# The start of a fused attention and MLP kernel in another order: one tile alone, its q ahead of v's last part, and other slots for the work behind it

## The chip, the core and the metric

The kernel runs on one core of a Trainium2 chip. The time is the device's own, in microseconds (us), one launch, lower is better; runs of one kernel mostly agree within 0.3%. The profile's span runs from the first to the last instruction of the core and is about 2 us shorter than the time.

Engines: PE is TensorE (matmul), PEld its weight loads, DVE is VectorE, ACT is ScalarE, POOL is GpSimd, which also issues the loads that cast float32 to bfloat16. Each engine works through its own list in program order.

## The reference

```python
kv  = einsum('bhsd,bhse->bhde', k, v)             # B=8, H=8, S=576, D=64, float32
o   = einsum('bhsd,bhde->bhse', q, kv)
x   = o / sqrt(mean(o*o, -1) + 1e-6) * g_norm     # then heads side by side: [8, 576, 512]
xn  = (x - mean(x)) / sqrt(var(x) + 1e-6) * g_ln
out = x + relu(xn @ w_ch1) @ w_ch2                # w_ch1 [512, 2048], w_ch2 [2048, 512]
```

## The kernel before

Per batch there are four tiles of 128 rows (0 to 3), and the remaining 64 rows of two batches make one tile more. A tile goes through: o (PE), square (ACT), sum `ss` (DVE), root `rms` (ACT), x and the scaled, centred `xc` (DVE), a transpose of `xc` (PE, "turn") and its copy to `xT_blk` (ACT). Then come the two layers. The division by the standard deviation is put off to the output addition `finish`.

The first layer of a batch is 16 groups of 16 matmuls, the second 64 long matmuls. Each group, and each four long matmuls, opens a *slot*; an agenda says what else is issued just before a slot (the comments in the code cuts are put in here; `...` marks what is left out):

```python
    def tick():                                   # called at the head of each slot
        for _, fn in sorted(agenda.pop(clock[0], []), key=lambda e: e[0]):
            fn()
        clock[0] += 1
    ...
    at(4, lambda: turn_first(3, ps_m, "misc"))
    at(5, lambda: t[3].o())
    at(5.1, x3)                                   # tile 3: square, ss, root, y, x, xc
    at(6, lambda: t[2].turn(True))                # tile 2's transpose and its copy by ACT
    ...
    at(21, lambda: kv_of(1))
    q_turns(23, 1)                                # batch 1: DVE copies q, then PE turns it
    for j, s, tn in ((0, 24, 30), (1, 27, 34), (2, 31, 38), (3, 35, 42)):
        plan_tile(s, lambda j=j: main_tile(1, j), tn, True)
```

`plan_tile(s, ..., tn)` issues o, square and ss at slot s, root, y, x and xc at slot s + 2, and the turn at slot tn. Batch 0's first layer has slots 0 to 15, its second layer 16 to 31, batch 1's first layer begins at slot 32, and the groups of batch 1's tile 1 begin at slot 36.

```python
    for ts, c0, c1 in ((0, 0, 8), (1, 0, 8), (0, 8, 12), (1, 8, 12), (0, 12, 16), (1, 12, 16),
                       (2, 0, 16), (3, 0, 16)):
        mm1(0, ts, 1, c0, c1)                     # tile ts; four chunks of w1 to a slot
    ...
    for ts in range(4):
        mm2_part(0, ts, p2s[ts], 0, nDe // 2)
    for ts in range(4):
        ...
        mm2_part(0, ts, p2, nDe // 2, nDe)
        finish(0, ts, p2)                         # DVE: the output addition
```

The start loads k (float32, on two other queues), then on POOL's queue v in two halves, q of the lower rows in two halves of heads, w1's first chunk, and the rest. Tiles 0 and 1 go through the start together, in two halves of heads.

## Time and profile before

| | before |
|---|---|
| time, median of 4 | 291.75 us (291.61 to 292.32) |
| span | 289.6 us |
| TensorE busy | 281.9 us, 97% |
| first first-layer matmul of batch 0 | 15.78 us |
| second group of the first layer | 18.25 us in the timeline; 18.42 in the view of the chain (`--critical`), which counts it from the end of what went before |
| second layer of batch 0 begins | 33.37 us |
| first layer of batch 1 begins | 50.39 us |

The page of the kernel before, part 1: busy us, share, instructions.

```profile
span 289.6 us, 5791 instructions
PE 281.9 (97%) x2312; PEld 158.6 (55%) x2312; DVE 151.0 (52%) x335; ACT 155.0 (54%) x339; POOL 41.0 (14%) x68
```

The waits of PE in the kernel before: who waited for whom, in all, how often, the longest.

```profile
engine line waited for: us in total, times, longest us
PE even L219 <- DMA v_in<-in_v_dram: 1.4, 2, 0.7
PE p L196 <- DVE eps_sb L137: 1.2, 1, 1.2
PE tp L541 <- DVE xc L532: 0.8, 1, 0.8
PE o_ps L260 <- DVE qt L191: 0.2, 1, 0.2
```

Every wait in this view ends before 18.1 us, and PE is busy for 97% of the span. From there on the matrix unit sets the time of the whole kernel: what delays it once is not won back, and there is little to shorten but the start. The view leaves out waits under 0.15 us by its count.

The timeline of PE before (start us, busy us, what, count; in brackets the wait just ahead). L402 is the first layer, L418 the second, L337 a tile's turn:

```profile
15.78 1.34 PE L402 MATMUL p<-xT_blk,w_sb 128*128 128x128 bf16 x16
17.05 0.44 PE L183 MATMUL tp<-identity,q_in 64*64 64x64 bf16 x16
...
18.25 2.84 PE L402 MATMUL p<-xT_blk,w_sb 128*128 128x128 bf16 x48
21.03 0.44 PE L183 MATMUL tp<-identity,q_in 64*64 64x64 bf16 x16
...
23.42 0.39 PE L337 MATMUL tp<-identity,xc 128*128 128x128 bf16 x4
23.65 3.06 PE L402 MATMUL p<-xT_blk,w_sb 128*128 128x128 bf16 x48
26.64 0.31 PE L183 MATMUL tp<-identity,q_in 64*64 64x64 bf16 x8
...
33.37 4.48 PE L418 MATMUL p<-w_sb,m 128*128 128x512 bf16 x20
...
52.18 0.39 PE L337 MATMUL tp<-identity,xc 128*128 128x128 bf16 x4
```

The lines of L183 are turns of batch 0's q. The line at 23.42 is tile 2's turn at slot 6. Slots 6 and 7 are other tiles' groups, and tile 2's own start only at slot 8, so ACT has two slots (1.8 us) to copy the turned tile. The timeline of ACT before:

```profile
22.51 0.60 ACT L405 ACTIVATE m<-p 128x512 bf16<-128x512 f32 x1 [0.30 <-PE p L402]
23.00 0.59 ACT L266 ACTIVATE sq<-o_ps 128x512 f32<-128x512 f32 x1
24.34 0.30 ACT L297 ACTIVATE rms<-ss,eps_sb 128x8 f32<-128x8 f32 x1 [0.75 <-DVE ss L287]
24.55 0.58 ACT L405 ACTIVATE m<-p 128x512 bf16<-128x512 f32 x1
25.03 0.58 ACT L339 COPY xT_blk<-tp 128x512 bf16<-128x512 bf16 x1
```

Tile 3's square and root stand in ACT's list ahead of the copy, and ACT stands still for 0.75 us until DVE has the sum. The copy ends at 25.61, 2.2 us after the turn was issued. Two slots do not quite hide it: the 48 matmuls at 23.65 took 3.06 us, where the 48 at 18.25 took 2.84, so PE already loses about 0.2 us at tile 2's first group.

The timeline of DVE before, around batch 1's tiles (L423 is the output addition, L287 a sum, L292 begins a tile's y, L321 is its xc):

```profile
44.41 0.75 DVE L423 SCALAR_TENSOR_TENSOR o_sb<-p,rstd,x_blk 128x512 f32<-128x512 f32 x1 [1.09 <-PE p L418]
...
47.63 0.68 DVE L287 TENSOR_REDUCE ss<-sq 128x8 f32<-128x512 f32 x1
48.23 0.74 DVE L423 SCALAR_TENSOR_TENSOR o_sb<-p,rstd,x_blk 128x512 f32<-128x512 f32 x1
...
50.76 0.75 DVE L321 SCALAR_TENSOR_TENSOR xc<-x_blk,st_blk,g_ln_sb 128x512 bf16<-128x512 f32 x1
```

DVE has no gap there, but tile 1's xc ends at 51.51, still before its turn at 52.18.

### The profile page before, as it was taken

Reading aid. Unit: us, or ns where it says so; the run is one execution under the profiler, and the core shown is the slowest. Engines: PE = TensorE matmul, PEld = TensorE weight load, DVE = VectorE, ACT = ScalarE, POOL = GpSimd, SP = SyncE. Lnnn points to the kernel's source line nnn. Section 1 sums busy time; section 2 is a strip of 40 time slices with the busy share of each in tenths; the row PEclk is TensorE's granted clock in tenths of the full one; section 3 lists DMA queues with packets and bytes.
Section 4 is the critical chain, followed back from the end, with each engine's and each line's share of the span. In section 5 each row is a group of like instructions: output and inputs, shape, how many; then the busy total and the mean of one; then the engine's idle time right before and its main releaser. Section 6 shows DMA issues by size and latency. Waiting matters only on the chain.

```text
span 289.6 us, 5791 instructions
## 1 busy us (share of the span) xinstructions
PE 281.9 (97%) x2312; PEld 158.6 (55%) x2312; DVE 151.0 (52%) x335; ACT 155.0 (54%) x339; POOL 41.0 (14%) x68
## 2 busy tenths in 40 slices
PE   7889999999999999999999999999999999999995
PEld 2579755996569644444444444444444444444444
DVE  5775028847997793765366925762578300220022
ACT  3467755885469832882189418920894076016500
POOL 8522520032032003200410023000000000000000
PEclk9999999999999999999999999999999999999999
DMA  7999999469999918995997179938202510131033
GB/s 215 203 206 203 201 202 218 109 99 188 155 177 160 151 40 158 205 167 102 148 208 103 42 146 194 178 75 164 54 18 53 112 36 0 38 81 28 0 74 73
DMA packets 64378, 36.10 MB, mean 125 GB/s; under 512 B 31836, under 2 KB 59356, under 8 KB 64352
## 3 DMA queue, kind: packets, MB, share of 16 engines
q0 software_dynamic: 28016, 17.76, 44.2%
q1 hardware_dynamic: 35824, 17.25, 30.5%
q10 hardware_dynamic: 512, 0.72, 0.7%
q8 instruction: 18, 0.29, 0.4%
q14 instruction: 8, 0.07, 0.1%
HBM read 36.71 MB, written 9.44 MB: 159 GB/s over the span
## 4 chain that ended last, share of the span: by engine, by line
PE 93%; DMA 2%; ACT 1%; DVE 1%; POOL 1%; issue 1%; POOLq 0%
PE p L418 43%; PE p L402 43%; PE o_ps L260 3%; DMA q_in<-in_q_dram 2%; PE kv_ps L235 2%; PE tp L183 1%; PE p L196 1%; PE tp L337 1%; ACT sq L266 0%; PE tp L170 0%; PE o_half L500 0%; POOL v_in L126 0%; ACT xT_blk L542 0%; ACT m L405 0%; DVE x_blk L278 0%
## 5 line engine op out<-in xcount | busy, mean ns | idle before, releaser
L402 PE MATMUL p<-xT_blk,w_sb 128*128 128x128 bf16 (+2 forms) x1024 | 131.8, 286 | 0.2
L418 PE MATMUL p<-w_sb,m 128*128 128x512 bf16 (+2 forms) x608 | 129.2, 368 | 0.0
L405 ACT ACTIVATE m<-p 128x512 bf16<-128x512 f32 x144 | 85.5, 596 | 43.3 <-PE p L402 41.1
L402 PEld LDWEIGHTS <-w_sb 128*128 128x128 bf16 x1024 | 78.5, 98 | 44.1 <-issue 0.6
L418 PEld LDWEIGHTS <-m 128*128 128x128 bf16 x608 | 56.8, 98 | 61.8
L423 DVE SCALAR_TENSOR_TENSOR o_sb<-p,rstd,x_blk 128x512 f32<-128x512 f32 (+2 forms) x38 | 27.4, 721 | 54.3 <-PE p L418 48.7
L266 ACT ACTIVATE sq<-o_ps 128x512 f32<-128x512 f32 x34 | 20.2, 595 | 41.5 <-PE o_ps L260 41.4
L287 DVE TENSOR_REDUCE ss<-sq 128x8 f32<-128x512 f32 x34 | 23.0, 678 | 11.2 <-ACT sq L266 11.2
L329 ACT ACTIVATE dev<-x_blk,st_blk 128x512 f32<-128x512 f32 x36 | 25.7, 714 | 4.6 <-DVE st_blk L315 4.4
L321 DVE SCALAR_TENSOR_TENSOR xc<-x_blk,st_blk,g_ln_sb 128x512 bf16<-128x512 f32 x34 | 25.6, 752 | 1.2
L292 DVE TENSOR_TENSOR y<-o_ps,inv 128x512 f32<-128x512 f32 x34 | 23.5, 692 | 3.0
L311 DVE SCALAR_TENSOR_TENSOR x_blk<-y,g_norm_sb 128x512 f32<-128x512 f32 x34 | 23.5, 692 | 1.2
L411 DVE RECIPROCAL rstd<-rstd 128x4 f32<-128x4 f32 x9 | 1.6, 174 | 35.3 <-ACT rstd L410 35.3
L304 DVE RECIPROCAL inv<-rms 128x8 f32<-128x8 f32 x36 | 7.2, 201 | 23.0 <-ACT rms L297 23.0
L98 POOL COPY gate<-qt 1x1 bf16<-1x1 bf16 x5 | 0.9, 178 | 114.1 <-DMA qt<-q_p 114.1
L297 ACT ACTIVATE rms<-ss,eps_sb 128x8 f32<-128x8 f32 x36 | 10.7, 297 | 9.5 <-DVE ss L287 8.8
L260 PEld LDWEIGHTS <-qt 128*128 128x128 bf16 (+1 forms) x152 | 9.9, 100 | 7.4 <-issue 1.7
L260 PE MATMUL o_ps<-kv_pack,qt 128*128 128x128 bf16 (+1 forms) x152 | 13.3, 220 | 0.2 <-DVE qt L191 0.2
L196 PE MATMUL p<-fill_sb 128*128 128x512 bf16 x28 | 8.1, 445 | 1.2 <-DVE eps_sb L137 1.2
L329 ACT ACTIVATION_READ_ACCUMULATOR dev<-x_blk,st_blk 128x1 f32 x36 | 6.9, 190 | 0.0
L235 PEld LDWEIGHTS <-k_in 128*64 128x64 bf16 x280 | 5.0, 112 | 2.6 <-issue 2.5
L238 ACT CAST kv_pack<-kv_ps 64x256 bf16<-64x256 f32 x7 | 2.6, 366 | 7.2 <-PE kv_ps L235 7.2
(79 smaller groups left out, 116.8 us busy)
## 6 DMA issues: line engine op xcount, KB each, us to landing
out_dram<-o_sb SPq DMA_DIRECT2D x70, 128.0 KB, 2.4
w_sb<-in_moe_w_ch_dram POOLq DMA_DIRECT2D x8, 512.0 KB, 13.8
k_in<-in_k_dram POOLq DMA_DIRECT2D x7, 320.0 KB, 5.8
v_in<-in_v_dram POOLq DMA_DIRECT2D x7, 320.0 KB, 9.4
q_in<-in_q_dram POOLq DMA_DIRECT2D x7, 320.0 KB, 12.7
q_in<-in_q_dram POOLq DMA_DIRECT2D x8, 256.0 KB, 12.7
k_in<-in_k_dram POOLq DMA_DIRECT2D x7, 256.0 KB, 7.3
v_in<-in_v_dram POOLq DMA_DIRECT2D x7, 256.0 KB, 11.3
```

The costliest lines, as they stand in the source:

```text
L196: nc.tensor.matmul(p1, lhsT=fill_sb[:, :128], rhs=fill_sb, start=True, stop=True)
L260: nc.tensor.matmul(flat[rows, hp * 128:(hp + 1) * 128], lhsT=lhsT_of(hp), rhs=kvp[:, hp, :], start=True, stop=True)
L266: nc.scalar.activation(self.sq_t, self.o_ps, func=AF.Square)
L287: nc.vector.tensor_reduce(self.ss, self.sq_t, axis=AX.X, op=ALU.add)
L292: nc.vector.tensor_mul(self.y_t, self.o_ps, self.inv().to_broadcast([128, H, D]))
L311: nc.vector.scalar_tensor_tensor(x_blk[:, ts].rearrange("p (h d) -> p h d", h=H), in0=self.y_t, scalar=1.0, in1=g_norm_sb.to_broadcast([12 ...
L321: nc.vector.scalar_tensor_tensor(self.xc_t, in0=x_blk[:, self.ts], scalar=st[:, 1, self.ts:self.ts + 1], in1=g_ln_sb, op0=ALU.add, op1=ALU ...
L329: nc.scalar.activation(dev, x_blk[:, ts], func=AF.Square, bias=st[:, 1, ts:ts + 1], accum_out=st[:, 2, ts:ts + 1])
L402: nc.tensor.matmul(p1[:, i, :], lhsT=w1_sb[:, kk, de * 128:(de + 1) * 128], rhs=blk[2][:, kk, sl], start=(kk == 0), stop=(kk == nK - 1))
L405: nc.scalar.activation(m1[:, de0:de0 + per, sl], p1, func=AF.Relu)
L418: nc.tensor.matmul(p2[:, c0:c1], lhsT=m1s[b][:, de, ts * 128:(ts + 1) * 128], rhs=w2_sb[:, de, c0:c1], start=(de == 0), stop=(de == nDe - 1))
L423: nc.vector.scalar_tensor_tensor(o_sb[:, c0:c1], in0=p2[:, c0:c1], scalar=rstds[b][:, ts:ts + 1], in1=blks[b][0][:, ts, c0:c1], op0=ALU.mu ...
```

## The change

Intent: get tile 0 alone to the first layer early, by loading its part of q before v's last head pair; lay the other q turns into its waits; order the first layer by w1's chunks as they land; and load w2's third chunk ahead of batch 1's q, so that the second layer, now in three parts, does not wait for w2. Because q of batch 1 then lands later, its turns and the tiles behind move to later slots.

```diff
-    nc.gpsimd.dma_start(v_p[:, :HP // 2], pairs(v, 0, HP // 2))
-    nc.gpsimd.dma_start(v_p[:, HP // 2:], pairs(v, HP // 2, HP))
-    for h0 in (0, H // 2):
-        nc.gpsimd.dma_start(q_in[0][:64, h0:h0 + H // 2], lo(q, 0, h0, h0 + H // 2))
+    nc.gpsimd.dma_start(v_p[:, :HP - 1], pairs(v, 0, HP - 1))
+    nc.gpsimd.dma_start(q_in[0][:64, :, :2], lo(q, 0)[:, :, :2])
+    nc.gpsimd.dma_start(v_p[:, HP - 1:], pairs(v, HP - 1, HP))
+    nc.gpsimd.dma_start(q_in[0][:64, :, 2:], lo(q, 0)[:, :, 2:])
 ...
-    load_batch(1)
+    load(k_in[1], k, 1)
+    load(v_in[1], v, 1)
     load_w2(2)
+    load(q_in[1], q, 1)
     load_w2(3)
 ...   (kv of batch 0 in three pairs and one instead of two halves; tile 0 alone through the
 ...    start; tile 1's turn, o and square behind it, its sum behind tile 0's xc; turns of q for
 ...    tiles 2 and 3 ahead of slot 1; tile 2 takes the o_g path, in which
 ...    PE makes a second product with kv already times g_norm, and DVE needs one step less for x)
+    at(1, before_1)
+    at(2, before_2)                 # tile 2: o_g, root, x, xc
+    at(4, before_4)                 # tile 3: o, square, ss, root, y, x, xc
     at(6, lambda: t[2].turn(True))
 ...
-    q_turns(23, 1)
-    for j, s, tn in ((0, 24, 30), (1, 27, 34), (2, 31, 38), (3, 35, 42)):
+    q_turns(25, 1)
+    for j, s, tn in ((0, 26, 31), (1, 29, 34), (2, 32, 38), (3, 35, 42)):
 ...
-    for ts, c0, c1 in ((0, 0, 8), (1, 0, 8), (0, 8, 12), (1, 8, 12), (0, 12, 16), (1, 12, 16),
-                       (2, 0, 16), (3, 0, 16)):
+    for ts, c0, c1 in ((0, 0, 4), (1, 0, 4), (0, 4, 8), (1, 4, 8), (0, 8, 12), (1, 8, 12),
+                       (2, 0, 12), (0, 12, 16), (1, 12, 16), (2, 12, 16), (3, 0, 16)):
 ...
-    for ts in range(4):
-        mm2_part(0, ts, p2s[ts], 0, nDe // 2)
+    for de0, de1 in ((0, nDe // 2), (nDe // 2, nDe * 3 // 4)):
+        for ts in range(4):
+            mm2_part(0, ts, p2s[ts], de0, de1)
 ...
-        mm2_part(0, ts, p2, nDe // 2, nDe)
+        mm2_part(0, ts, p2, nDe * 3 // 4, nDe)
         finish(0, ts, p2)
```

More of the change, by code (lines that the diff above doesn't have):

```diff
@@ L191, in turn_first, with fill @@
         copy(qts[0][:, i, :, :n], tp[:, :, :n])
-    def fill(n, pool=ps2, tag="p2"):
+    def fill(n, p1=None):
+        if p1 is None:
+            p1 = ps2.tile([128, 512], f32, tag="p2", name="p1")
         for _ in range(n):
-            p1 = pool.tile([128, 512], f32, tag=tag, name="p1")
             nc.tensor.matmul(p1, lhsT=fill_sb[:, :128], rhs=fill_sb, start=True, stop=True)
-            del p1
+        return p1
     def turn_q_dma(b):
@@ L205, in turn_q_dma, with __init__, mms, copies @@
         qts[b] = q_t
-    def kv_first():
-        kvp = held[0] = kv_pack[0]
-        g = g_norm_sb.to_broadcast([128, HP // 2, D])
-        for i, (pe, te, po, to) in enumerate(((ps_m, "misc", ps1, "p1"), (ps1, "p1", ps1, "p1"))):
-            even = pe.tile([128, HP // 2, D], f32, tag=te, name="even")
-            odd = po.tile([128, HP // 2, D], f32, tag=to, name="odd")
-            hps = slice(i * HP // 2, (i + 1) * HP // 2)
-            for hp in range(hps.start, hps.stop):
+    class KvFirst:
+        def __init__(self, hp0, hp1, pools):
+            self.hps, self.pools = slice(hp0, hp1), pools
+        def mms(self):
+            n = self.hps.stop - self.hps.start
+            (pe, te), (po, to) = self.pools
+            self.even = pe.tile([128, n, D], f32, tag=te, name="even")
+            self.odd = po.tile([128, n, D], f32, tag=to, name="odd")
+            for hp in range(self.hps.start, self.hps.stop):
                 for j in range(JP):
                     js = slice(j * D, (j + 1) * D)
-                    for hh, dst in ((0, even), (1, odd)):
+                    for hh, dst in ((0, self.even), (1, self.odd)):
                         rows = slice(hh * D, hh * D + D)
-                        nc.tensor.matmul(dst[rows, hp - hps.start, :], lhsT=k_p[rows, hp, js],
-                                         rhs=v_p[rows, hp, js],
+                        nc.tensor.matmul(dst[rows, hp - self.hps.start, :],
+                                         lhsT=k_p[rows, hp, js], rhs=v_p[rows, hp, js],
                                          start=(j == 0), stop=(j == JP - 1))
-            nc.vector.tensor_copy(kvp[:D, hps, :D], even[:D])
-            nc.scalar.copy(kvp[D:, hps, D:], odd[D:])
-            nc.vector.tensor_mul(kv_g[:D, hps, :D], even[:D], g[:D])
-            nc.vector.tensor_mul(kv_g[D:, hps, D:], odd[D:], g[D:])
-            del even, odd
+        def copies(self):
+            nc.vector.tensor_copy(kv_pack[0][:D, self.hps, :D], self.even[:D])
+            nc.scalar.copy(kv_pack[0][D:, self.hps, D:], self.odd[D:])
+        def times_g(self):
+            g = g_norm_sb.to_broadcast([128, self.hps.stop - self.hps.start, D])
+            nc.vector.tensor_mul(kv_g[:D, self.hps, :D], self.even[:D], g[:D])
+            nc.vector.tensor_mul(kv_g[D:, self.hps, D:], self.odd[D:], g[D:])
+            del self.even, self.odd
     def kv_of(b):
@@ L474 @@
     qts[0] = qt_pool.tile([128, JJ, HP, 128], bf16, tag="qt", name="qt")
+    held[0] = kv_pack[0]
     fill(18)
-    kv_first()
-    t = [main_tile(0, i, ps2, "p2") for i in range(4)]
-    for i in range(2):
-        t[i].ss = work.tile([128, H, 1], f32, tag="ss", bufs=4, name="ss")
-    sqs = [work.tile([128, H, D], f32, tag="sq", name="sq") for _ in range(2)]
-    banks = (((ps_out, "ops"), (ps_m, "misc")), ((ps_out, "ops"), (ps1, "p1")))
-    copies = ((nc.scalar.copy, nc.scalar.copy), (nc.vector.tensor_copy, nc.vector.tensor_copy))
@@ L486, in half_turn @@
-    def half_turn(half):
-        hp0 = half * HP // 2
-        tps = [ps2.tile([128, HP // 2, 128], bf16, tag="p2", name="tp") for _ in range(2)]
-        for i in range(2):
-            turn_groups(tps[i], i, 2 * hp0, 2 * hp0 + H // 2)
-        for i in range(2):
-            copies[half][i](qts[0][:, i, hp0:hp0 + HP // 2], tps[i])
-    def half_o(i, half):
-        hp0 = half * HP // 2
-        pool, tag = banks[half][i]
-        o = pool.tile([128, H // 2, D], f32, tag=tag, name="o_half")
-        flat = o.rearrange("p h e -> p (h e)")
-        for k2 in range(HP // 2):
-            nc.tensor.matmul(flat[:, k2 * 128:(k2 + 1) * 128], lhsT=qts[0][:, i, hp0 + k2, :],
-                             rhs=kv_pack[0][:, hp0 + k2, :], start=True, stop=True)
-        nc.scalar.activation(sqs[i][:, half * H // 2:(half + 1) * H // 2], o, func=AF.Square)
@@ L504, in half_red @@
-    def half_red(i, half):
-        hs = slice(half * H // 2, (half + 1) * H // 2)
-        nc.vector.tensor_reduce(t[i].ss[:, hs], sqs[i][:, hs], axis=AX.X, op=ALU.add)
-    half_turn(0)
-    fill(2, ps_out, "ops")
-    half_o(0, 0)
-    half_turn(1)
-    half_o(1, 0)
-    half_o(0, 1)
-    half_red(0, 0)
-    half_red(0, 1)
-    half_o(1, 1)
-    t[0].root()
-    half_red(1, 0)
-    half_red(1, 1)
-    t[0].o_g(ps1, "p1")
+    kv_a = KvFirst(0, HP - 1, ((ps_m, "misc"), (ps1, "p1")))
+    kv_b = KvFirst(HP - 1, HP, ((ps1, "p1"), (ps1, "p1")))
@@ new lines, with part_o @@
+    t = [main_tile(0, 0)] + [main_tile(0, i, *((ps1, "p1") if i == 1 else (ps2, "p2")))
+                             for i in range(1, 4)]
+    t[0].ss = work.tile([128, H, 1], f32, tag="ss", bufs=4, name="ss")
+    sq_0 = work.tile([128, H, D], f32, tag="sq", name="sq")
+    o_0 = {}
+    def part_o(kv_x):
+        hp0, hp1 = kv_x.hps.start, kv_x.hps.stop
+        o_0[hp0] = ps_out.tile([128, 2 * (hp1 - hp0), D], f32, tag="ops", name="o_part")
+        flat = o_0[hp0].rearrange("p h e -> p (h e)")
+        for hp in range(hp0, hp1):
+            nc.tensor.matmul(flat[:, (hp - hp0) * 128:(hp - hp0 + 1) * 128],
+                             lhsT=qts[0][:, 0, hp, :], rhs=kv_pack[0][:, hp, :],
+                             start=True, stop=True)
@@ new lines, in part_sq, with part_red @@
+    def part_sq(kv_x):
+        hp0, hp1 = kv_x.hps.start, kv_x.hps.stop
+        nc.scalar.activation(sq_0[:, 2 * hp0:2 * hp1], o_0.pop(hp0), func=AF.Square)
+    def part_red(kv_x):
+        hs = slice(2 * kv_x.hps.start, 2 * kv_x.hps.stop)
+        nc.vector.tensor_reduce(t[0].ss[:, hs], sq_0[:, hs], axis=AX.X, op=ALU.add)
+    kv_a.mms()
+    kv_a.copies()
+    turn_first(0, ps2, "p2")
+    kv_a.times_g()
+    fill(2)
+    kv_b.mms()
+    kv_b.copies()
+    part_o(kv_a)
+    part_o(kv_b)
+    part_sq(kv_a)
@@ L521 @@
+    part_sq(kv_b)
+    kv_b.times_g()
+    part_red(kv_a)
+    part_red(kv_b)
+    turn_first(1, ps_m, "misc")
+    t[0].root()
+    t[0].o_g(ps2, "p2")
+    dead = fill(2)
+    t[1].o()
+    t[1].sq()
+    turn_first(J, ps_m, "misc")
     t[1].o_g(ps1, "p1")
-    fill(8)
+    fill(3, dead)
+    del dead
     t[0].x_g()
-    t[1].root()
     def halves_xc(i):
@@ L534, in halves_xc, with half_turn, before_1, before_2 @@
             yield xc
-    def halves_turn(i, xcs, pool, tag):
-        xT = t[i].blk[2]
-        for c, xc in enumerate(xcs):
-            tp = pool.tile([128, 2, 128], bf16, tag=tag, name="tp")
-            for kk in range(2):
-                nc.tensor.transpose(tp[:, kk, :], xc[:, kk * 128:(kk + 1) * 128], identity)
-            nc.scalar.copy(xT[:, 2 * c:2 * c + 2, i * 128:(i + 1) * 128], tp)
-    halves_turn(0, halves_xc(0), ps_out, "ops")
+    def half_turn(i, c, xc, copy):
+        tp = ps_out.tile([128, 2, 128], bf16, tag="ops", name="tp")
+        for kk in range(2):
+            nc.tensor.transpose(tp[:, kk, :], xc[:, kk * 128:(kk + 1) * 128], identity)
+        copy(t[i].blk[2][:, 2 * c:2 * c + 2, i * 128:(i + 1) * 128], tp)
+    for c, xc in enumerate(halves_xc(0)):
+        half_turn(0, c, xc, nc.scalar.copy)
+    t[1].red()
     t[1].x_g()
     xc1 = list(halves_xc(1))
-    def x2():
+    def before_1():
+        turn_first(2, ps_m, "misc")
+        tp = ps2.tile([128, HP, 128], bf16, tag="p2", name="tp")
+        turn_groups(tp, 3, 0, H)
+        half_turn(1, 0, xc1[0], nc.scalar.copy)
+        t[2].o()
+        half_turn(1, 1, xc1[1], nc.vector.tensor_copy)
+        t[2].sq()
+        nc.scalar.copy(qts[0][:, 3], tp)
         t[2].red()
-        t[2].y()
-        t[2].x()
+        del tp, xc1[:]
+    def before_2():
+        t[2].o_g(ps2, "p2")
+        t[2].x_g()
         t[2].xc()
-    def x3():
+    def before_4():
+        t[3].o()
         t[3].sq()
@@ L560, in x3 @@
         t[3].xc()
-    def o2():
-        t[2].o()
-        t[2].sq()
     def next_loads():
@@ L569, in next_loads @@
         load_batch(2)
-    at(1, lambda: turn_first(2, ps_m, "misc", nc.vector.tensor_copy))
-    at(1.1, lambda: halves_turn(1, xc1, ps_out, "ops"))
-    at(1.2, o2)
-    at(1.3, x2)
-    at(4, lambda: turn_first(3, ps_m, "misc"))
-    at(5, lambda: t[3].o())
-    at(5.1, x3)
+    at(1, before_1)
+    at(2, before_2)
+    at(4, before_4)
     at(6, lambda: t[2].turn(True))
-    at(9, lambda: turn_first(J, ps_m, "misc"))
     at(9.5, next_loads)
```

## The prediction

> **What bounds it now.** TensorE, busy 281.9 of 289.6 us (page, part 1). The waits view: 3.6 us of waiting, all before 18.1 us. The chain of waits runs from q's first half landing (9.76 us) through VectorE (reductions, x_blk, xc) to the first first-layer matmul of batch 0 (L402, 15.78 us); from 18.42 us nearly all matmul. So the start can give about 2 us at most; any new TensorE wait later is added in full.
>
> **The change, costed from the trace.**
> 1. q's first two groups now follow three v pairs. A v pair takes 0.71 us to land (halves at 7.50 and 8.92). I estimate v's three pairs at 8.25, q at 9.2, v's last pair at 9.9, q's rest at 11.0. The Trainium skill (DMA: Bandwidth & Descriptors, Specifications) asks 512 B for line rate; the new q rows are 256 and 384 B. The trace has 640 B packets at 0.069 us, 512 B at 0.060; I allow 0.3 us delay for later loads.
> 2. Tile 0 alone: one reduction pair less ahead of it on VectorE. First L402 at 14.6-15.0: gain about 1 us.
> 3. Tile 1's reduction (0.69), root (0.30) and x_blk (about 0.9) now follow tile 0, and the second matmul group is tile 1's. Its transposed input is ready at about 18.3; the second group (tile 0's) started at 18.42 before. So the gain of 2 is spent. Turns 3 and J (0.61 us) fall into that wait; tile 2's o_g costs 0.22.
> 4. Tile 2's turn stays at slot 6, now tile 2's own matmuls (before: slot 8). ScalarE must first do tile 3's square, wait for its reduction, do its root and two Relus, then the copy. Before: square 23.00, copy done 25.61. ScalarE is strict FIFO (skill, TensorE: Matmul & The Clock Gate, engine queue depths; the trace agrees, 0.75 us wait). With one more Relu (0.49) in front, TensorE waits about 1.6 us. Batch 0's first layer ends about 34.2, not 33.37.
> 5. The second layer's four output additions (L423, 0.68 us each, two slots apart) now come in successive slots (28-31), between batch 1's tiles 0 and 1, while tile 1 starts two slots later (29) with its turn still at 34. VectorE, without a gap from 44.4 to 57 us before, has 0.69 + 3 x 0.68 + 2.6 us to do before tile 1's xc: TensorE waits about 2 us at slot 34.
> 6. w2's third chunk earlier: no wait for w2 exists now (lands 39.83, used 42.04); no gain.
>
> These durations laid in program order on each engine (the kernel before so comes within 0.3 us at 33 us): +0.9 us by the end of the first layer, +2 at slot 34, shaded to +2.4.
>
> **Predicted: 294.2 us, 80% range 291.0 to 295.6.** Faster by over 2%: 0.01; within 2%: 0.97; slower by over 2%: 0.02.
>
> **What would show it.** Right: first L402 before 15.2; a TensorE wait of 0.5-1 us before the second group; one of 1-2 us on ScalarE's xT_blk near 24-25.5 us; another of 1-2.5 us on VectorE's xc near 53-56 us, with three L423 in a row before tile 1's y. Wrong: TensorE without waits between 19 and 60 us, or the second layer starting before 33.3.
>
> **What would make it wrong.** q landing much earlier or later; ScalarE reaching tile 2's copy sooner; batch 1's root 0 coming sooner; w1's chunks (17.91, 20.46, 23.07 now) being a hidden limit.

## The result, and the profile after

| | before | after |
|---|---|---|
| time, median of 4 | 291.75 us (291.61 to 292.32) | 293.93 us (293.81 to 294.62) |
| ratio | | 1.0076 (95%: 1.0055 to 1.0097) |

Ratios are the mean time of one kernel's runs over that of the other's in the same rounds, so they are not quite the ratios of the medians quoted. The change makes the kernel 0.8% slower, which at a threshold of 2% still counts as the same.

The first profile of the changed kernel was of its slowest run (294.62 us): one of the 16 shares of v's first load landed at 8.89 us, the other fifteen by 8.10, and that share stayed about 0.8 us behind in the next loads. A second set of six runs of the same kernel (293.95 us, 293.81 to 294.08) had no such straggler in its profiled run. The lines below are of that second profile, with a span of 292.1 us; lines are shifted by the edit, so that the first layer is L414, the second L430, a turn L349, the addition L435.

The waits of PE in the kernel after:

```profile
engine line waited for: us in total, times, longest us
PE tp L349 <- DVE xc L333: 1.6, 1, 1.6
PE p L414 <- ACT xT_blk L351: 1.4, 1, 1.4
PE p L199 <- DVE eps_sb L137: 1.2, 1, 1.2
PE tp L555 <- DVE xc L548: 0.9, 2, 0.5
PE even L226 <- DMA v_in<-in_v_dram: 0.2, 1, 0.2
```

The first two are new. The timeline of PE after shows where they lie:

```profile
14.89 1.34 PE L414 MATMUL p<-xT_blk,w_sb 128*128 128x128 bf16 x16
16.16 0.70 PE L185 MATMUL tp<-identity,q_in 64*64 64x64 bf16 x32
17.25 0.28 PE L555 MATMUL tp<-identity,xc 128*128 128x128 bf16 x2 [0.39 <-DVE xc L548]
...
18.00 1.26 PE L414 MATMUL p<-xT_blk,w_sb 128*128 128x128 bf16 x16
...
23.11 0.39 PE L349 MATMUL tp<-identity,xc 128*128 128x128 bf16 x4
24.94 3.73 PE L414 MATMUL p<-xT_blk,w_sb 128*128 128x128 bf16 x64 [1.44 <-ACT xT_blk L351]
...
34.09 4.48 PE L430 MATMUL p<-w_sb,m 128*128 128x512 bf16 x20
...
51.11 1.95 PE L414 MATMUL p<-xT_blk,w_sb 128*128 128x128 bf16 x32
54.70 0.40 PE L349 MATMUL tp<-identity,xc 128*128 128x128 bf16 x4 [1.63 <-DVE xc L333]
```

The first group comes 0.89 us earlier (14.89 for 15.78), the second only 0.25 us (18.00 for 18.25), because it is now tile 1's and tile 1 comes late. After two of its matmuls it waits for the second half of tile 1's input, which DVE has copied at 18.26; in the view of the chain the group runs from 18.32, for 18.42 before. Nearly all of the gain is gone there. Behind tile 2's turn at 23.11 PE stands still for 1.44 us by the view's count, which begins at the modelled end of the turn; from start to start it loses 1.60 us (23.11 to 24.94, for 23.42 to 23.65 before). The second layer begins at 34.09, 0.72 us later than before. The second wait, 1.63 us at 54.70, comes before the turn of batch 1's tile 1; that turn is 2.52 us later than before (54.70 for 52.18). From start to start this wait costs 1.80 us (51.11 to 54.70, for 50.39 to 52.18). Nothing after it changes the distance: the spans differ by 2.5 us (292.1 for 289.6). The times differ by 2.2, since time less span is 2.1 us for the kernel before and 1.8 for this one; where that 0.3 us lies the profile does not show.

The timeline of ACT after, at the first wait:

```profile
21.80 0.59 ACT L278 ACTIVATE sq<-o_ps 128x512 f32<-128x512 f32 x1
23.14 0.30 ACT L309 ACTIVATE rms<-ss,eps_sb 128x8 f32<-128x8 f32 x1 [0.75 <-DVE ss L299]
23.35 1.06 ACT L417 ACTIVATE m<-p 128x512 bf16<-128x512 f32 x2
24.30 0.58 ACT L351 COPY xT_blk<-tp 128x512 bf16<-128x512 bf16 x1
```

It is the picture of before with one Relu more: square, 0.75 us of standing still for the sum, root, two Relus, copy. The copy ends at 24.88 and PE goes on at 24.94. What two slots of other work had all but hidden is now in the open, because the next group in PE's list is tile 2's own.

The timeline of DVE after, at the second wait:

```profile
49.44 0.74 DVE L435 SCALAR_TENSOR_TENSOR o_sb<-p,rstd,x_blk 128x512 f32<-128x512 f32 x1
50.11 0.68 DVE L299 TENSOR_REDUCE ss<-sq 128x8 f32<-128x512 f32 x1
50.70 1.40 DVE L435 SCALAR_TENSOR_TENSOR o_sb<-p,rstd,x_blk 128x512 f32<-128x512 f32 x2
52.02 0.19 DVE L316 RECIPROCAL inv<-rms 128x8 f32<-128x8 f32 x1
...
53.89 0.75 DVE L333 SCALAR_TENSOR_TENSOR xc<-x_blk,st_blk,g_ln_sb 128x512 bf16<-128x512 f32 x1
```

Three additions and the sum stand before tile 1's inv, y, x and xc. Its xc ends at 54.64 and PE's turn begins at 54.70.

### The profile page after: what moved, and what is told of

The parts are those of the page before. It is cut to its first block, busy times and chain, and to the rows that moved or that the text cites. A ratio compares the mean times of both kernels' runs of the same rounds, so it can differ in the third digit from the quotient of the medians.

```text
span 292.8 us, 5758 instructions
## 1 busy us (share of the span) xinstructions
PE 280.8 (96%) x2286; PEld 158.8 (54%) x2313; DVE 149.9 (51%) x331; ACT 155.8 (53%) x338; POOL 40.8 (14%) x68
## 3 DMA queue, kind: packets, MB, share of 16 engines
q1 hardware_dynamic: 35824, 17.25, 30.6%
## 4 chain that ended last, share of the span: by engine, by line
PE 89%; DVE 4%; DMA 3%; ACT 2%; issue 1%; DVEq 0%; POOLq 0%
PE p L414 41%; PE p L430 41%; PE o_ps L272 3%; DMA v_in<-in_v_dram 3%; PE kv_ps L247 2%; DVE o_sb L435 1%; DVE xc L333 1%; PE tp L349 1%; DVE x_blk L323 0%; DVE x_blk L290 0%; DVE y L304 0%; DVE ss L299 0%; ACT m L417 0%; ACT sq L278 0%; ACT qt L175 0%
## 5 line engine op out<-in xcount | busy, mean ns | idle before, releaser
L414 PE MATMUL p<-xT_blk,w_sb 128*128 128x128 bf16 (+2 forms) x1017 | 131.3, 285 | 2.1 <-ACT xT_blk L351 1.4
L430 PE MATMUL p<-w_sb,m 128*128 128x512 bf16 (+2 forms) x590 | 126.8, 368 | 1.6 <-issue 1.0
L414 PEld LDWEIGHTS <-w_sb 128*128 128x128 bf16 x1024 | 78.5, 98 | 45.5 <-issue 2.3
L430 PEld LDWEIGHTS <-m 128*128 128x128 bf16 x608 | 56.9, 98 | 61.9
L435 DVE SCALAR_TENSOR_TENSOR o_sb<-p,rstd,x_blk 128x512 f32<-128x512 f32 (+2 forms) x38 | 27.3, 721 | 53.2 <-PE p L430 50.3
L278 ACT ACTIVATE sq<-o_ps 128x512 f32<-128x512 f32 x35 | 20.8, 594 | 41.5 <-PE o_ps L272 41.4
L299 DVE TENSOR_REDUCE ss<-sq 128x8 f32<-128x512 f32 x35 | 23.7, 678 | 10.2 <-ACT sq L278 10.2
L304 DVE TENSOR_TENSOR y<-o_ps,inv 128x512 f32<-128x512 f32 x33 | 22.8, 692 | 3.0
L323 DVE SCALAR_TENSOR_TENSOR x_blk<-y,g_norm_sb 128x512 f32<-128x512 f32 x33 | 22.8, 692 | 1.1
L351 ACT COPY xT_blk<-tp 128x512 bf16<-128x512 bf16 x8 | 4.7, 583 | 3.5 <-PE tp L349 3.5
```

The lines of the kernel that those rows point to most:

```text
L278: nc.scalar.activation(self.sq_t, self.o_ps, func=AF.Square)
L299: nc.vector.tensor_reduce(self.ss, self.sq_t, axis=AX.X, op=ALU.add)
L304: nc.vector.tensor_mul(self.y_t, self.o_ps, self.inv().to_broadcast([128, H, D]))
L323: nc.vector.scalar_tensor_tensor(x_blk[:, ts].rearrange("p (h d) -> p h d", h=H), in0=self.y_t, scalar=1.0, in1=g_norm_sb.to_broadcast([12 ...
L414: nc.tensor.matmul(p1[:, i, :], lhsT=w1_sb[:, kk, de * 128:(de + 1) * 128], rhs=blk[2][:, kk, sl], start=(kk == 0), stop=(kk == nK - 1))
L430: nc.tensor.matmul(p2[:, c0:c1], lhsT=m1s[b][:, de, ts * 128:(ts + 1) * 128], rhs=w2_sb[:, de, c0:c1], start=(de == 0), stop=(de == nDe - 1))
```

## The experiments

Twelve runs. Each was timed in five rounds beside the kernel before; the kernel before had medians of 291.68 to 291.80 us.

| run | time, us | ratio to before (95%) |
|---|---|---|
| after_again | 293.95 | 1.0071 (1.0058 to 1.0084) |
| tile2_later | 292.41 | 1.0021 (1.0007 to 1.0035) |
| slots_back | 292.50 | 1.0022 (1.0008 to 1.0036) |
| additions_back | 293.45 | 1.0055 (1.0040 to 1.0069) |
| layer2_alone | 293.21 | 1.0056 (1.0042 to 1.0069) |
| slots_alone | 292.86 | 1.0031 (1.0012 to 1.0050) |
| split_alone | 291.76 | 1.0007 (0.9994 to 1.0020) |
| w2_alone | 292.41 | 1.0024 (1.0011 to 1.0037) |
| loads_back | 296.20 | 1.0162 (1.0137 to 1.0186) |
| tile3_behind | 294.37 | 1.0090 (1.0077 to 1.0104) |
| mended_w2_ahead | 292.38 | 1.0022 (1.0010 to 1.0034) |
| both_mended | 290.55 | 0.9965 (0.9952 to 0.9977) |

**after_again.** No edit.

> The changed kernel, unaltered. In its first profile one of the 16 DMA engines ran about 0.75 us behind the other fifteen from v's first load on (first load: fifteen shares by 8.10 us, the last at 8.89), and that run was 0.7 us slower than the other three. If that was a chance of the one run: all shares of v's first load within 0.4 us, first L414 at 14.8 to 15.1 us instead of 15.63, time 293.8 to 294.0. If the small q rows (256 and 384 B) bring the straggler with them: it is there again and L414 starts at 15.6.

The straggler was a chance of the one run: the shares of v's first load landed between 7.78 and 8.13 us, the first group began at 14.89, and the median is that of the first set. The small rows of q do not bring it about.

**tile2_later: the wait before slot 6.**

```diff
-                       (2, 0, 12), (0, 12, 16), (1, 12, 16), (2, 12, 16), (3, 0, 16)):
+                       (0, 12, 16), (1, 12, 16), (2, 0, 16), (3, 0, 16)):
```

> The changed kernel with tile 2's three first-layer groups put back behind the last chunk of tiles 0 and 1 (slot 8 instead of 6). Theory (ScalarE, held by tile 3's root, is late with tile 2's copy): TensorE's wait of 1.4 to 1.6 us before slot 6 goes, no other takes its place, 1.4 to 1.6 us faster than the changed kernel, 292.3 us. Rival (tile 2 was put there because the last chunk of w1, which lands at 23.07 us, was late): TensorE waits for w1 at slot 6 (about 23.3 us) and at most 0.5 us is won.

The wait went and 1.5 us with it. PE's timeline runs through the place, although w1's last chunk landed only at 23.27 us in this run, just 0.3 us before it was used:

```profile
23.36 0.39 PE L349 MATMUL tp<-identity,xc 128*128 128x128 bf16 x4
23.58 3.74 PE L414 MATMUL p<-xT_blk,w_sb 128*128 128x128 bf16 x64
```

So moving tile 2's groups back is enough to remove the first wait. Had PE got there more than 0.3 us earlier, the chunk of w1 would have been the limit; putting tile 2 in front was a guard against that, and in this run it was not needed.

**tile3_behind: why the copy is late.**

```diff
-    at(4, before_4)
     at(6, lambda: t[2].turn(True))
+    at(6.5, before_4)
```

> The changed kernel with tile 3's product, square, root and the rest issued just behind tile 2's turn at slot 6, instead of at slot 4; the order of the matmul groups stays. Theory (tile 3's root stands in ScalarE's queue in front of tile 2's copy): the wait before slot 6 falls from 1.4 to about 0.7 us (Relu and copy remain), and a new one of about 0.7 us comes before tile 3's turn at slot 10, so that the time stays within 0.3 us of the changed kernel. Rival (the copy is late for another reason, the distance of one slot alone): the wait before slot 6 stays at 1.4 us.

The wait before slot 6 halved and another came before tile 3's turn, as expected:

```profile
24.25 3.73 PE L414 MATMUL p<-xT_blk,w_sb 128*128 128x128 bf16 x64 [0.71 <-ACT xT_blk L351]
28.55 0.40 PE L349 MATMUL tp<-identity,xc 128*128 128x128 bf16 x4 [0.57 <-DVE xc L333]
```

Half of the wait is thus tile 3's square and root ahead of the copy in ACT's list; the other half is one Relu and the copy itself; no run takes these two apart. The old place of tile 2's groups hides both halves, this order only moves one of them. The median is 0.4 us above the changed kernel's, a little more than the 0.3 allowed, and the second layer begins at 34.15 for 34.09; what the four runs add beyond that was not traced.

**slots_back, additions_back: the wait before tile 1's turn.** In slots_back only batch 1's slots are those of before; in additions_back only the second layer's order.

```diff
-    q_turns(25, 1)                                                              # slots_back
-    for j, s, tn in ((0, 26, 31), (1, 29, 34), (2, 32, 38), (3, 35, 42)):
+    q_turns(23, 1)
+    for j, s, tn in ((0, 24, 30), (1, 27, 34), (2, 31, 38), (3, 35, 42)):
```

```diff
-    for de0, de1 in ((0, nDe // 2), (nDe // 2, nDe * 3 // 4)):                  # additions_back
-        for ts in range(4):
-            mm2_part(0, ts, p2s[ts], de0, de1)
+    for ts in range(4):
+        mm2_part(0, ts, p2s[ts], 0, nDe // 2)
 ...
-        mm2_part(0, ts, p2, nDe * 3 // 4, nDe)
+        mm2_part(0, ts, p2, nDe // 2, nDe)
```

> The changed kernel with batch 1's q turns and tiles 0 to 2 in the slots of before (turns 23; tiles 24/30, 27/34, 31/38), the additions still in four successive slots. Theory A (tile 1 has only five slots from its product to its turn): the wait of 1.6 us before tile 1's turn near 55 us goes, 1.6 to 2.2 us faster than the changed kernel, 291.8 us; q of batch 1 lands about 39.9, just before its turn at slot 23. Theory B (the four additions in a row hold VectorE): the wait stays, above 1 us, 293.5 or more.

> The changed kernel with only the second layer's order of before: after the first half each tile's other eight products run together, so that the additions L435 are two slots apart; batch 1's tiles keep the new slots. Theory A: most of the loss stays, because tile 1's slots are the cause; the first addition now comes before tile 0's y, so two waits of about 0.6 and 0.9 us stand for the one of 1.6 to 2.0: 0.3 to 0.7 us faster than the changed kernel, 293.4 us. Theory B: the wait goes, 1.6 us faster, 292.3 us.

With the old slots no wait on xc is left in the layers, with the additions still in a row; 1.5 us were won instead of 1.6 to 2.2. DVE's copy of q ended only at 41.31, and PE, free at about 41.06, turned it at 41.37, so some 0.3 us went there (41.06 is an estimate: eight matmuls of 0.216 us from 39.33 on). With the old additions and the new slots two smaller waits stand for the one, 0.25 us before tile 0's turn and 0.68 before tile 1's (0.6 and 0.9 were expected), and only 0.5 us is won. Theory A held in both.

**slots_alone, split_alone, layer2_alone: the same on the kernel before.** The edits are those above the other way round: the new slots alone; the three parts of the second layer alone; both, with w2's third chunk ahead of q as well.

> The kernel before with only the new slots of batch 1's turns and tiles (turns 25; tiles 26/31, 29/34, 32/38); additions two slots apart, w2 in its old place. Theory (the slots are the cause, the additions in a row make it larger): two waits of TensorE on xc, about 0.25 us before tile 0's turn and 0.7 before tile 1's, as in the changed kernel with the additions put back: 292.6 to 292.8 us. Rival (only slots and additions together make a wait): no wait, 291.75 us.

> The kernel before with only the second layer's three parts, so that the four additions come in four successive slots, and batch 1's tiles in their old slots. Theory A (the slots of tile 1 are the cause of the wait near 55 us, the additions alone do nothing): 291.75 us, no wait of TensorE on xc. Theory B (the additions in a row hold VectorE): a wait of over 0.5 us before one of the turns, 292.3 us or more.

> The kernel before with only the later parts of the change: w2's third chunk ahead of q of batch 1, the second layer in three parts, batch 1's turns and tiles in the new slots. Theory: TensorE waits 1.6 to 2 us before tile 1's turn as in the changed kernel, since the cause lies wholly there: 293.4 to 293.9 us. Rival (the wait comes only because the first layer is late and shifts the stages against each other): 291.8 us.

The four additions in a row cost nothing by themselves (291.76 us). The new slots alone cost about 1 us (the median is 0.06 above the range expected), with the same two waits, 0.25 and 0.68. Both together have one wait of 1.63, just as in the changed kernel. The first two lines are of slots_alone, the third is of layer2_alone:

```profile
50.87 0.40 PE L337 MATMUL tp<-identity,xc 128*128 128x128 bf16 x4 [0.25 <-DVE xc L321]
54.82 0.40 PE L337 MATMUL tp<-identity,xc 128*128 128x128 bf16 x4 [0.68 <-DVE xc L321]
55.41 0.40 PE L339 MATMUL tp<-identity,xc 128*128 128x128 bf16 x4 [1.63 <-DVE xc L323]
```

The median of layer2_alone rose by 1.5 us, 0.2 less than the least expected. Its span rose by 1.8 (291.4 for 289.5 to 289.7): as in the changed kernel, 0.3 us less time lies outside the span. So the second wait is independent of the start; its cause is tile 1's five slots from product to turn, and the additions in a row turn two waits of together 0.9 us into one of 1.6. The profiled runs of slots_alone and layer2_alone were slowed by something else as well, told at the end; their medians were not. That of split_alone began its first group 0.7 us late (16.49).

**w2_alone, mended_w2_ahead: w2's third chunk.** The first is the kernel before with only the loads in the new order; the second is the mended kernel below with it.

```diff
-    load_batch(1)
+    load(k_in[1], k, 1)
+    load(v_in[1], v, 1)
     load_w2(2)
+    load(q_in[1], q, 1)
     load_w2(3)
```

> The kernel before with w2's third chunk ahead of q of batch 1, and nothing else. In the changed kernel's trace this order makes q's copy start at 40.7 us (37.44 before) and end at 41.5; in the kernel before q's first turn is at 40.27. Theory (the chunk's new place is no gain by itself and forces the later turns, which then squeeze tile 1): TensorE waits about 1 to 1.3 us for the copy of q before the turns at slot 23, 292.7 to 293.0 us. Rival (as the prediction had it: no gain and no loss): 291.75 us.

> The mended kernel (290.55 us) with w2's third chunk ahead of q of batch 1 again. Theory: the copy of q ends at about 41.4 us, while its turn at slot 23 now comes at 39.4: TensorE waits 1.7 to 2.0 us, 292.3 to 292.6 us. Rival: w2's chunk was late in the mended kernel without showing, and its new place pays: 290.5 or less.

The order costs 0.6 us in the kernel before (0.3 less than expected: q's copy began at 39.97, not 40.7, and the turns came at 40.86 for 40.27) and 1.8 in the mended one, where the start is earlier and PE waits longer for q. The line of PE in mended_w2_ahead:

```profile
41.24 0.62 PE L172 MATMUL tp<-identity,q_p 128*128 128x128 bf16 x8 [1.54 <-DVE q_p L609]
```

The chunk's new place removes no wait, it delays q; by the intent told above, the later turns were the answer to that, and they squeezed tile 1. They won nothing back: with the chunk ahead, the mended start takes 292.38 us with the old slots (mended_w2_ahead) and 292.41 with the new ones (tile2_later).

**loads_back: where the early start comes from.** The changed kernel with the four first loads of before.

> The changed kernel with the first loads of before (v in halves, then q in two halves of heads). The parts then need all of v (8.9 us) and all of q (10.7 us). Theory (the early start comes from the order of the loads): first L414 at 16.5 us or later instead of 14.9, 1.4 to 1.8 us slower than the changed kernel, 295.5 us. Rival (it comes from tile 0 being alone on VectorE): less than 0.5 us slower.

The median rose by 2.3 us. The order of the loads is needed for the early start; tile 0 alone on DVE does not give it. (The reverse, the new loads with both tiles together, was not run.) The size was missed, 1.4 to 1.8 us were expected. The profiled run, 297.31 us, is no measure of it: PE waited for q's second half (landed at 10.93), was then granted half the clock (mean 0.50 from 13 to 17 us in the windows view), and its first group began at 18.09 us instead of 14.89. The five times spread from 295.22 to 297.43. The fastest, with a mean clock of 1.000, is 1.3 us above the changed kernel; but the median run had a clock of 0.999, so the clock explains only part of the spread, and the rest is open.

**both_mended: what is left when both waits are gone.** The changed kernel with tile2_later's order of groups, the old slots, and w2's third chunk behind q again.

> The changed kernel with tile 2's groups at slot 8 again, batch 1's turns and tiles in the slots of before, and q of batch 1 loaded ahead of w2's third chunk again (in the new order q would come too late for its turn at slot 23, which the faster first layer brings to about 40 us). What is left of the change: the start, and the second layer in three parts. Theory (the two waits were the whole loss, and the start is worth about 1 us once they are gone): no TensorE wait between 19 and 60 us, second layer begins at about 32.5 us instead of 33.37, 290.7 us, faster than the kernel before by 0.8 to 1.2. Rival (the start gains nothing, because tile 1 comes late): 291.7 us.

290.55 us, 0.35% faster than the kernel before (inside the 2% that count as the same, but clear of noise), and the best of all. The second layer begins at 32.51 us, 0.86 earlier than before, and the span is 288.7 for 289.6. So the new start is worth 0.9 us. The first group gains as much, but these are not the same microseconds: PE's timeline at the second group is that of the changed kernel (18.01), where about 0.1 is left. What counts is work that left the first layer: the two turns of q at 21.03 and 26.64 (0.44 and 0.31 us) now lie in waits of the start, that of the remaining rows at 12.38 and tile 3's at 16.18, in the wait for tile 1. The 0.2 us before tile 2's groups are won too, and tile 2's o_g costs about as much. This is read from the timelines; no run moves those turns alone.

With this the sum closes: 1.60 and 1.80 us lost at the two waits, less 0.86 won, is 2.54, and the span of the changed kernel is 2.5 us longer.

## Why the prediction was right

The measured 293.93 us lies 0.3 us from the predicted 294.2.

1. *The loads.* Landings were close: v's three pairs 8.13 (8.25 predicted), q's first part 8.98 (9.2), v's last pair 9.58 (9.9), q's rest 10.71 (11.0). The 0.3 us allowed for small rows did not show: w1's first chunk landed at 13.11 us, 13.19 before.
2. *Tile 0 alone, about 1 us.* Right: first group at 14.89, predicted 14.6 to 15.0. Loads_back shows that the order of the loads is needed for it, so the reason given in this point, one pair of sums less on DVE, is not enough by itself; point 1 of the prediction has the loads.
3. *Tile 1 eats the gain.* Right nearly to the figure: in the view of the chain, from which the prediction took 18.42, the second group now runs from 18.32; 18.3 was predicted. The wait in front of it was put at 0.5 to 1 us; the view lists 0.39, at 17.25. It also laid the turns of q for tile 3 and for the remaining rows into this wait; tile 3's lies there (16.16), the other still earlier (12.36), and from them comes most of both_mended's gain.
4. *Tile 2's copy, 1.6 us.* 1.60 from start to start, 1.44 in the view, at 24.94 us where 24 to 25.5 was named; shown by tile2_later and tile3_behind. The second layer began at 34.09, predicted 34.2.
5. *Tile 1's xc, 2 us at slot 34.* 1.80 from start to start, 1.63 in the view. DVE's work was right: 5.3 us were summed (0.69 + 3 x 0.68 + 2.6), and from the first addition at 49.44 to the end of xc at 54.64 it took 5.2. The text named two causes side by side. The experiments part them: the slots are the cause (about 1 us alone), the additions in a row only enlarge it and cost nothing alone.
6. *w2's chunk, nothing to gain.* True but short: the order costs 0.6 us alone and forced the slots of point 5. That loss was in reach of the prediction, since the trace of before shows that q was turned at 40.27 with its copy done at 38.25, a margin of 2.0 us, and the chunk takes 2.5 us to land.

The number itself owes something to luck. The terms add up to 2.9 us; they were shaded to 2.4 without a reason given. The spans differ by 2.5, and the times by only 2.2 because 0.3 us less lies outside the span, which the prediction did not foresee. Unshaded, the prediction would have been about 0.7 us too high.

The Trainium skill (TensorE: Matmul & The Clock Gate, engine queue depths) calls ScalarE and VectorE strict FIFO; point 4 rests on it, and both traces agree: ACT stands still 0.75 us for a sum, although PE had finished the input of the Relu behind it.

## What to carry to other kernels

When a pipeline is bound by one engine from early on, an earlier start is worth only what reaches that engine's list without a hole behind it: after a reorder, look at each handover that stayed in its slot while its consumer moved, since an in-order engine exposes at once what two slots of other work had all but hidden. Look too at what can be laid into the waits of the start: here two turns of q, 0.75 us of work, were most of what the new start won. Lay the measured durations in program order on each engine, check that it gives the old kernel's times, then read the new waits from it; here that found both of them, the place and nearly the size. And before moving a load ahead, find the wait it removes; if there is none, it only delays what it overtook, and the repairs of that delay cost more.

## What the Trainium skill lacked or had wrong

- *DMA: Bandwidth & Descriptors, Specifications* asks transfers of at least 512 B for line rate. Here q's rows went from 640 B to 256 and 384 B (packets 0.041 and 0.051 us for 0.069, so 0.092 for the pair), and yet w1's first chunk behind them landed at 13.11 us against 13.19. A packet's time was no measure of the queue's pace in this stage; why is open.
- *DMA: Bandwidth & Descriptors* names engines that are usually slower, but not a single delay in one run: one share of 16 fell 0.8 us behind in v's first load (8.89 against 8.10) and stayed behind, and that run was 0.7 us longer. In the one profile taken of the six runs that followed it was not there, and all six times were below 294.1. The trace does not name the DMA engine.
- *TensorE: Matmul & The Clock Gate, the HAM clock gate* puts the fall to half clock at an idle window of about 3.4 us (a later section names frequent short idles too, without a size). In layer2_alone PE was granted 0.50 from 18 to 21 us, while busy, though its longest wait between 3 and 18 us was 1.0 us. From 13 to 17 us it was busy for 2.86; so was the profiled run of the kernel before, which kept a clock of 1.00. What decides it the traces do not show. In the rounds of the experiments, runs of the kernel before at a mean clock of 0.993 to 0.994 took 292.85 to 293.01 us, the others 291.60 to 292.03. So this kernel has two times, about 1.2 us apart, and small edits of its start should be compared by medians of several runs with their clocks.
- *Runtime: NRT & Kernel Launch* breaks down what surrounds a kernel, but does not tell what makes it differ between near-equal kernels. The part of the time outside the span was 2.1 to 2.2 us in the kernel before, split_alone and w2_alone, and 1.7 to 1.9 in all the others; the cause is open.
